# Top-k attention with an MLP behind it: tails of two batches taken together, an even flow of MLP chunks, and two short lists merged by one scan

## The chip, the cores and the metric

The kernel runs on one core of one Trainium2 chip. The metric is the device time of one execution in microseconds (us). TensorE (PE) multiplies, VectorE (DVE), ScalarE (ACT) and GpSimd (POOL) work on vectors, SyncE (SP) issues the transfers.

## What is computed

The reference is sparse attention whose output is fed to an MLP. All arrays are float32.

```python
q, k, v: (8, 8, 576, 64)                       # batch, heads, sequence, head size
scores = matmul(q, k^T) / 8
kth    = 32nd largest score of each row
scores = where(scores >= kth, scores, -1e9)
attn   = softmax(scores)
x      = matmul(attn, v) -> (4608, 512)        # the heads side by side
h      = x @ w_in                              # 512 -> 2048
g      = 0 if h <= -1, h if h >= 1, else (h + 1)^2 / 4
out    = g @ w_out                             # 2048 -> 512
```

## The kernel before

**Steps.** The rows of a batch are cut into four blocks of 128 and a tail of 64. A step takes one block of queries for two heads, so that its score tile is 128 x 2 x 576; for a tail, a step takes two pairs of heads, since 64 rows of two heads fill the 128 partitions. A block has four steps, a tail two, which makes 18 per batch and 144 in all. The list `rounds` (L462-L470) gives the order of blocks: of each two batches the four blocks of the first, its tail, the four blocks of the second, its tail; only for the last two batches do both tails come together.

**What a step does.** TensorE computes the scores (`scores`, L257-L271), ScalarE copies them to SBUF as `s`. VectorE finds the 32nd largest value of each row (`first_top`, L282-L294, and `weights`, L297-L347). It halves the work with pairs: `more` is the larger of columns c and c + 288 (L279); the 32 largest of `more` come by four rounds of MAX8 with MATCH_REPLACE8 between them (L290, L306, L315), in `tops`, falling. Then `more` is overwritten with the smaller of each pair (L317) and its eight largest are `seconds` (L320). The two lists have to be merged: L321 takes the elementwise smaller of `seconds` and the eight values of `tops` just ahead of the last, in reverse order, and L324 takes the largest of these and the 32nd of `tops`, once for each of the two lists. That is the threshold `kth`. L330 keeps the exponentials at or above it and sums them; L335 and L336 give the reciprocal of the sum. ScalarE makes the exponentials ahead of that (L291, L293), GpSimd scales them (L343) and notes by how much the eighth of `seconds` exceeds the threshold (L345); if that ever happened, a second, plain version of the whole computation would run behind the first.

**From weights to the MLP.** The scaled weights are transposed by a transfer (`move_w`, L368-L375) or, in the first and the last steps, by TensorE (`transpose_w`, L351-L364). `values` (L381-L404) multiplies them with v into `xT`, the MLP's input. When the steps of all tiles of a chunk are through, the chunk's MLP is pending (L606-L608): 16 slices of the hidden layer, each with L419 on TensorE, L423 and L431 on ScalarE, L436 to L438 on GpSimd, and L444 on TensorE four slices behind. A chunk is one tile of 128 rows or a pair of tiles; two tails of 64 rows make one tile. Pairs use products with 256 columns at L419, single tiles 128. In the last chunk, VectorE takes over GpSimd's part (L426-L430).

**Who orders the work.** Everything on the four compute engines runs in the order in which the program is written, and a planner in the kernel writes it. For each step it goes through seven slots (L629-L669). In each it emits a part of the top-k work, perhaps scores, values or transposes of neighbouring steps, and then calls `advance` (L516-L532) with an allowance of products. An allowance is counted in units of a 128 x 128 x 128 product; a tile has 128 units, and `pending` pieces are emitted while the amount due covers their cost. The allowance per step, `share`, is all the products not yet emitted, of ready and of future chunks, over the steps that are left (L619). `K_TIME` (L513) is the planner's idea of the length of a step on VectorE. During the first 14 steps or so the weights w_in and w_out are also converted piece by piece.

```python
            share = (total - spent) / (n + 2 - m)
...
                advance((EARLY_SHARE if early else share) / SLOTS if m < n else 32.0, now)
```

Of the kernel before, what the change touches and what calls it, by code (L numbers as in the profile page):

```python
# [10 lines left out]
F32 = mybir.dt.float32  # L11
# [13 lines left out]
def kernel(  # L25
# [10 lines left out]
    nc = tc.nc  # L36
    B, H, S, D = q.shape
    NTOK, DM = out.shape
    DFF = moe_w_in.shape[1]
    P = 128  # L40
# [4 lines left out]
    NT = S // P  # L45
# [6 lines left out]
    NK = DM // P  # L52
    NF = DFF // P
# [5 lines left out]
    const = ctx.enter_context(tc.tile_pool(name="const", bufs=1))  # L59
# [18 lines left out]
    for i in range(2):  # L78
        v_tails.append([const.tile([P, H, D], F32, name=f"v_tail{i}{x}") for x in range(2)])
        for x in v_tails[i]:  # L80
            nc.gpsimd.memset(x, 0.0)

# [5 lines left out]
    excess = const.tile([P, 2 * n_steps + n_pieces], F32, name="excess")  # L88
# [68 lines left out]
    def run(ctx, paired):  # L157
        xtp = ctx.enter_context(tc.tile_pool(name="xtp", bufs=3))
        stage = ctx.enter_context(tc.tile_pool(name="stage", bufs=2))
        att = ctx.enter_context(tc.tile_pool(name="att", bufs=2))  # L160
# [96 lines left out]
        def scores(st):  # L257
            t, hp, kT, qT = st["t"], st["hp"], st["keys"]["kT"], st["qT"]
            st["s"] = s = att.tile([P, 2, S], F32, name="s", bufs=3)
            for hf in range(2):  # L260
# [9 lines left out]
                                             start=True, stop=True)  # L270
                nc.scalar.activation(s[:, :, c0:c1], sp[:, :, 0:SH], AF.Copy, scale=SCALE)  # L271

        def pairs(st):
            s = st["s"]
            st["more"] = more = att.tile([P, 2, SH], F32, name="more")
            nc.vector.tensor_tensor(out=more, in0=s[:, :, 0:SH], in1=s[:, :, SH:S], op=ALU.max)  # L279


        def first_top(st):  # L282
            s = st["s"]
            if paired:
                pairs(st)
            st["tops"] = tops = att.tile([P, 2, TOP_K + 8], F32, name="tops", bufs=3)
            st["e"] = e = att.tile([P, 2, S], F32, name="e", bufs=3)
            nmax = att.tile([P, 2], F32, name="nmax")
            for i in range(2):
                nc.vector.max(out=tops[:, i, 0:8], in_=(st["more"] if paired else s)[:, i, :])  # L290
            nc.scalar.activation(nmax, tops[:, :, 0], AF.Copy, scale=-1.0)  # L291
            for i in range(2):
                nc.scalar.activation(e[:, i, :], s[:, i, :], AF.Exp, bias=nmax[:, i:i + 1])  # L293
                yield  # L294


        def weights(st, after):  # L297
            s, m, tops, e = st["s"], st["m"], st["tops"], st["e"]
            kth = att.tile([P, 2, 8], F32, name="kth", bufs=3)
            if paired:  # L300
                src = rest = less = st["more"]
            else:
                src, rest = s, att.tile([P, 2, S], F32, name="rest", bufs=1)
            for r in range(8, TOP_K, 8):
                for i in range(2):
                    nc.vector.match_replace(out=rest[:, i, :], in_to_replace=tops[:, i, r - 8:r],  # L306
                                            in_values=src[:, i, :], imm_value=LOWEST)
                src = rest
                if r == 8:
                    yield  # L310
                if r + 8 == TOP_K:
                    yield
                    yield from first_top(after) if after is not None else (None, None)
                for i in range(2):
                    nc.vector.max(out=tops[:, i, r:r + 8], in_=src[:, i, :])  # L315
            if paired:
                nc.vector.tensor_tensor(out=less, in0=s[:, :, 0:SH], in1=s[:, :, SH:S], op=ALU.min)  # L317
                seconds = att.tile([P, 2, 8], F32, name="seconds")
                for i in range(2):
                    nc.vector.max(out=seconds[:, i, :], in_=less[:, i, :])  # L320
                nc.vector.tensor_tensor(out=tops[:, :, TOP_K:TOP_K + 8], in0=tops[:, :, TOP_K - 2:TOP_K - 10:-1],  # L321
                                        in1=seconds, op=ALU.min)
                for i in range(2):
                    nc.vector.max(out=kth[:, i, :], in_=tops[:, i, TOP_K - 1:TOP_K + 8])  # L324
                last = kth[:, :, 0]
            else:
                last = tops[:, :, TOP_K - 1]
            z = att.tile([P, 2], F32, name="z")
            for i in range(2):
                nc.vector.scalar_tensor_tensor(out=e[:, i, :], in0=s[:, i, :], scalar=last[:, i:i + 1],  # L330
                                               in1=e[:, i, :], op0=ALU.is_ge, op1=ALU.mult,
                                               accum_out=z[:, i:i + 1])
            yield
            rz = att.tile([P, 2], F32, name="rz")
            nc.vector.tensor_scalar(z, z, 1e-9, None, ALU.add)  # L335
            nc.vector.reciprocal(rz, z)  # L336
            if st["by_tensor"]:
                st["rz"] = diag = (late or words).tile([P, 2, P], F32, name="diag", bufs=1)
                for i in range(2):
                    nc.scalar.activation(diag[:, i, :], ident, AF.Copy, scale=rz[:, i:i + 1])  # L340
            else:
                for i in range(2):
                    nc.gpsimd.tensor_scalar(e[:, i, :], e[:, i, :], rz[:, i:i + 1], 1.0, ALU.mult, ALU.mult)  # L343
            if paired:
                nc.gpsimd.tensor_tensor(out=excess[:, 2 * m:2 * m + 2], in0=seconds[:, :, 7], in1=kth[:, :, 0],  # L345
                                        op=ALU.subtract)
            yield  # L347

# [113 lines left out]
        rounds, chunks = [], []  # L462
        for b in range(0, B, 2):
            a, c, tl = [(b, t) for t in range(NT)], [(b + 1, t) for t in range(NT)], (b, NT)
            if b + 2 < B:
                rounds += a + [tl] + c + [(b + 1, NT)]
                chunks += [a[0:2], a[2:4], c[0:2], c[2:4], [tl]] if b else [[x] for x in a + c + [tl]]
            else:
                rounds += a + [tl, (b + 1, NT)] + c
                chunks += [a[0:2], a[2:4], [tl]] + [[x] for x in c]  # L470
        steps = []
        for b, t in rounds:
            tile_of = (b, t) if t < NT else (b - b % 2, t)
# [4 lines left out]
        n = len(steps)  # L478

        ready = {max(m for m in range(n) if steps[m][3] == ch): ch for ch in range(len(chunks))}  # L480
# [4 lines left out]
        pending = deque()  # L485
        total, spent = sum(len(tiles) for tiles in chunks) * (NK * NF + NF * DM // P), 0
# [23 lines left out]
                inspected += 1  # L510


        K_TIME, PIECE_TIME, UNIT_TIME, SLOTS, EARLY_STEPS, EARLY_SHARE = 10.2, 0.55, 0.218, 7, 4, 32  # L513
        pe_time, dve_time, done, scored, ready_at, usable = 9.0, 12.0, {}, {}, {}, {0: 0.0}

        def advance(amount, until):  # L516
# [95 lines left out]
        for m in range(n + 2):  # L612
# [3 lines left out]
            elif not early and late is None:  # L616
                conversion.close()
                late = ctx.enter_context(tc.tile_pool(name="late", bufs=1))
            share = (total - spent) / (n + 2 - m)  # L619
            top_k, parts = None, [0] * SLOTS  # L620
            if m < n:
                top_k = weights(state[m], state[m + 1] if m + 1 < n else None)
                parts = [1] * SLOTS if early else [1, 1, 0, 1, 1, 1, 1]
                start = max(dve_time, scored[m])
                now_converting = range(SLOTS) if m < EARLY_STEPS else range(0, SLOTS, 2)
                dve_time = start + K_TIME + PIECE_TIME * min(len(now_converting), n_pieces - converted)
                done[m] = dve_time
                state[m]["by_tensor"] = early or m >= n - 2
# [93 lines left out]
```

## Time and profile before

The median of three runs is 1683.67 us (1682.41 to 1685.46). The profiled execution has a span of 1683.5 us.

| engine | busy us | share of the span |
|---|---|---|
| VectorE | 1550.5 | 92% |
| TensorE, products | 1549.2 | 92% |
| ScalarE | 1188.2 | 71% |
| TensorE, weight loads | 1050.8 | 62% |
| GpSimd | 974.8 | 58% |

The costliest groups of VectorE are L306 with 375.6 us, L315 with 348.9 and L330 with 242.0; L321 has 32.6 us in 144 instructions and L324 34.6 us in 288. Of TensorE, L419 has 594.1 us and L444 564.3. In the page, matmuls are pipelined and their ends are modelled, so that a record's duration is no price; the distance from the start of one record to the start of the next is. A product in float32 leaves two records. A group line has the line number, engine, operation, what is written and read with shapes, the count, then busy time and mean duration. A line of the timeline begins with the start and the duration in us; "x8" are eight records merged. A line of waits names who waited for whom, then us in total, times, and the longest.

### The profile page before, as it was taken

Reading aid. Unit: us, or ns where it says so; the run is one execution under the profiler, and the core shown is the slowest. Engines: PE = TensorE matmul, PEld = TensorE weight load, DVE = VectorE, ACT = ScalarE, POOL = GpSimd, SP = SyncE. Lnnn points to the kernel's source line nnn. Section 1 sums busy time; section 2 is a strip of 40 time slices with the busy share of each in tenths; the row PEclk is TensorE's granted clock in tenths of the full one; section 3 lists DMA queues with packets and bytes.
Section 4 is the critical chain, followed back from the end, with each engine's and each line's share of the span. In section 5 each row is a group of like instructions: output and inputs, shape, how many; then the busy total and the mean of one; then the engine's idle time right before and its main releaser. Section 6 shows DMA issues by size and latency. Waiting matters only on the chain.

```text
span 1683.5 us, 30910 instructions
## 1 busy us (share of the span) xinstructions
PE 1549.2 (92%) x9645; PEld 1050.8 (62%) x9645; DVE 1550.5 (92%) x4875; ACT 1188.2 (71%) x2552; POOL 974.8 (58%) x1720
## 2 busy tenths in 40 slices
PE   5586999999998899979999999979999999999998
PEld 4464666666665666646566766646566666666675
DVE  6999999999999999999999999999999999999922
ACT  5677677777777767777677877767667877767743
POOL 4675677666665554536465755526465765657750
PEclk6698999999998999979999999979999999999999
DMA  9333345455555546554555555554555544544400
GB/s 246 114 98 91 86 132 160 129 151 141 140 154 156 144 135 174 142 157 135 146 159 143 150 142 151 158 158 124 155 150 151 143 131 130 132 133 117 114 27 16
DMA packets 439055, 227.83 MB, mean 135 GB/s; under 512 B 393056, under 2 KB 401248, under 8 KB 438880
## 3 DMA queue, kind: packets, MB, share of 16 engines
q1 hardware_dynamic: 438880, 225.75, 49.4%
q8 instruction: 78, 1.28, 0.3%
q14 instruction: 97, 0.79, 0.2%
HBM read 62.91 MB, written 86.11 MB: 89 GB/s over the span
## 4 chain that ended last, share of the span: by engine, by line
DVE 51%; PE 33%; ACT 7%; issue 3%; POOL 3%; DMA 2%; SPq 1%; DVEq 0%; POOLq 0%; ACTq 0%
PE ph L419 13%; DVE more L306 12%; PE py L444 12%; DVE tops L315 10%; DVE e L330 8%; DVE more L317 4%; DVE seconds L320 4%; DVE tops L290 4%; DVE more L279 4%; PE po L389 3%; PE sp L269 3%; ACT halves L372 2%; ACT e L293 1%; DVE z L335 1%; DVE kth L324 1%
## 5 line engine op out<-in xcount | busy, mean ns | idle before, releaser
L419 PEld LDWEIGHTS ph<-xT,w_in 128*128 128x128 f32 x3328 | 505.1, 195 | 199.0 <-issue 88.5
L419 PE MATMUL ph<-xT,w_in 128*128 128x128 f32 (+1 forms) x3328 | 594.1, 326 | 32.8 <-ACT g L431 18.6
L444 PE MATMUL py<-w_out,g 128*128 128x512 f32 x1152 | 564.3, 605 | 2.0 <-POOL w_out L136 1.8
L423 ACT ACTIVATE r<-ph,half 128x128 f32<-128x128 f32 (+1 forms) x416 | 169.7, 408 | 292.9 <-PE ph L419 237.6
L306 DVE MATCH_REPLACE8 more<-tops,more 128x288 f32<-128x288 f32 x864 | 375.6, 442 | 0.0
L436 POOL TENSOR_SCALAR r<-r 128x128 f32<-128x128 f32 (+1 forms) x392 | 164.9, 421 | 343.4 <-ACT r L423 342.1
L315 DVE MAX8 tops<-more 128x8 f32<-128x288 f32 x864 | 348.9, 445 | 0.0
L343 POOL TENSOR_SCALAR e<-e,rz 128x576 f32<-128x576 f32 x260 | 211.9, 825 | 205.2 <-DVE rz L336 205.2
L372 ACT COPY halves<-e 128x1152 uint16<-128x1152 uint16 x260 | 286.9, 1156 | 14.7 <-POOL e L343 14.0
L444 PEld LDWEIGHTS py<-w_out,g 128*128 128x128 f32 x1152 | 197.4, 191 | 145.9 <-issue 117.8
L438 POOL TENSOR_TENSOR g<-r,g 128x128 f32<-128x128 f32 (+1 forms) x400 | 261.6, 654 | 31.4
L330 DVE SCALAR_TENSOR_TENSOR e<-s,kth,e 128x576 f32<-128x576 f32 x288 | 242.0, 877 | 0.5
L437 POOL TENSOR_TENSOR r<-r 128x128 f32<-128x128 f32 (+1 forms) x392 | 219.0, 559 | 32.7
L293 ACT ACTIVATE e<-s,nmax 128x576 f32<-128x576 f32 x288 | 218.4, 771 | 4.8
L269 PE MATMUL sp<-kT,qT 64*128 64x288 f32 x1024 | 169.0, 447 | 9.9 <-ACT kT L229 9.1
L271 ACT ACTIVATE s<-sp 128x576 f32<-128x576 f32 x288 | 170.0, 642 | 6.6 <-PE sp L269 6.4
L389 PE MATMUL po<-wT,v_in 128*64 128x128 f32 x2048 | 148.5, 287 | 22.1 <-DMA wT<-rows 13.9
L389 PEld LDWEIGHTS po<-wT,v_in 128*64 128x64 f32 x2048 | 115.5, 141 | 80.7 <-issue 18.3
L431 ACT ACTIVATE g<-ph,minus 128x128 f32<-128x128 f32 (+1 forms) x400 | 162.4, 406 | 0.0
L269 PEld LDWEIGHTS sp<-kT,qT 64*128 64x128 f32 x1024 | 91.8, 193 | 84.6 <-issue 40.6
L320 DVE MAX8 seconds<-more 128x8 f32<-128x288 f32 x288 | 118.3, 452 | 13.9
L317 DVE TENSOR_TENSOR more<-s 128x576 f32<-128x576 f32 x144 | 122.4, 850 | 4.9
(88 smaller groups left out, 1349.6 us busy)
## 6 DMA issues: line engine op xcount, KB each, us to landing
rows<-halves SPq DMA_DIRECT2D x130, 576.0 KB, 2.8
raw<-in_moe_w_out_dram SPq DMA_DIRECT2D x52, 256.0 KB, 3.0
raw<-in_moe_w_in_dram SPq DMA_DIRECT2D x48, 256.0 KB, 3.1
k_in<-in_k_dram SPq DMA_DIRECT2D x64, 128.0 KB, 2.9
q_in<-in_q_dram SPq DMA_DIRECT2D x32, 256.0 KB, 3.1
v_in<-in_v_dram SPq DMA_DIRECT2D x8, 1024.0 KB, 6.0
out_dram<-y SPq DMA_DIRECT2D x32, 256.0 KB, 2.6
kT<-in_moe_w_in_dram SPq DMA_DIRECT2D x16, 256.0 KB, 4.5
```

Of the source, the lines that this page charges most:

```text
L269: nc.tensor.matmul(o[:, a0 - c0:a1 - c0], qT[d, g, :], kT[d, g, k0:k0 + a1 - a0], start=True, stop=True)
L293: nc.scalar.activation(e[:, i, :], s[:, i, :], AF.Exp, bias=nmax[:, i:i + 1])
L306: nc.vector.match_replace(out=rest[:, i, :], in_to_replace=tops[:, i, r - 8:r], in_values=src[:, i, :], imm_value=LOWEST)
L315: nc.vector.max(out=tops[:, i, r:r + 8], in_=src[:, i, :])
L330: nc.vector.scalar_tensor_tensor(out=e[:, i, :], in0=s[:, i, :], scalar=last[:, i:i + 1], in1=e[:, i, :], op0=ALU.is_ge, op1=ALU.mult, acc ...
L343: nc.gpsimd.tensor_scalar(e[:, i, :], e[:, i, :], rz[:, i:i + 1], 1.0, ALU.mult, ALU.mult)
L372: nc.scalar.copy(halves[:, :, i * S:(i + 1) * S], st["e"][:, i, :].bitcast(U16).rearrange("p (k t) -> p t k", t=2))
L389: nc.tensor.matmul(po[j * D:(j + 1) * D], v_in[:, h, c, :] if c < NT else v_tl[0][:, h, :], wT[:, block(j, c)], start=(c == 0), stop=(c == ...
L419: nc.tensor.matmul(ph, w_in[:, kk, f * P:(f + 1) * P], xT[:, kk, c0:c1], start=(kk == 0), stop=(kk == NK - 1))
L437: nc.gpsimd.tensor_tensor(out=r, in0=r, in1=r, op=ALU.mult)
L438: nc.gpsimd.tensor_tensor(out=g, in0=r, in1=g, op=ALU.add)
L444: nc.tensor.matmul(pys[i], gs[f][:, i * P:(i + 1) * P], w_out[:, f, :], start=(f == 0), stop=(f == NF - 1))
```

## The change

Four things. The tails of two batches are now taken one behind the other everywhere, after the four blocks of the first, so that the tile they share is ready in the middle of the two batches rather than at their end. The chunks are cut anew: of the four pairs of batches, the first and the last have single tiles throughout, the second has pairs, the third has pairs in its first batch and single tiles in its second. The allowance `share` gets an upper limit, so that what is ready lasts until the next chunk is ready, and the same for every later chunk. And the two lists are merged by one scan: `tops` of the two rows of a step are laid out so that the end of the first list and the second half of the second lie side by side, `seconds` gets a large value in front of each list and is read backwards, and a scan with max and then min runs over 25 elements; its elements 8 and 24 are the two thresholds.

```diff
+    SPLIT = TOP_K // 2
+    LAST = SPLIT + 8
+    second_lists = [const.tile([P, LAST + 1], F32, name=f"seconds{i}") for i in range(2)]
+    for x in second_lists:
+        nc.gpsimd.memset(x, LOWEST)
+        for i in range(2):
+            nc.gpsimd.memset(x[:, i * SPLIT:i * SPLIT + 1], LARGEST)
...
+        def eight(tops, i, r):
+            c = (r // SPLIT * 2 + i) * SPLIT + r % SPLIT
+            return tops[:, c:c + 8]
...
-            nc.scalar.activation(nmax, tops[:, :, 0], AF.Copy, scale=-1.0)
+            nc.scalar.activation(nmax, tops[:, 0:2 * SPLIT:SPLIT], AF.Copy, scale=-1.0)
...
                 for i in range(2):
-                    nc.vector.max(out=seconds[:, i, :], in_=less[:, i, :])
-                nc.vector.tensor_tensor(out=tops[:, :, TOP_K:TOP_K + 8], in0=tops[:, :, TOP_K - 2:TOP_K - 10:-1],
-                                        in1=seconds, op=ALU.min)
-                for i in range(2):
-                    nc.vector.max(out=kth[:, i, :], in_=tops[:, i, TOP_K - 1:TOP_K + 8])
-                last = kth[:, :, 0]
+                    nc.vector.max(out=seconds[:, (1 - i) * SPLIT + 1:(1 - i) * SPLIT + 9], in_=less[:, i, :])
+
+                nc.vector.tensor_tensor_scan(out=kth, data0=tops[:, 2 * TOP_K - 1 - LAST:2 * TOP_K], data1=seconds[:, LAST::-1],
+                                             initial=LOWEST, op0=ALU.max, op1=ALU.min)
+                last = [kth[:, 8:9], kth[:, LAST:LAST + 1]]
...
-            if b + 2 < B:
-                rounds += a + [tl] + c + [(b + 1, NT)]
-                chunks += [a[0:2], a[2:4], c[0:2], c[2:4], [tl]] if b else [[x] for x in a + c + [tl]]
+            rounds += a + [tl, (b + 1, NT)] + c
+            if 0 < b and b + 2 < B:
+                chunks += [a[0:2], a[2:4], [tl]] + ([c[0:2], c[2:4]] if b + 4 < B else [[x] for x in c])
             else:
-                rounds += a + [tl, (b + 1, NT)] + c
-                chunks += [a[0:2], a[2:4], [tl]] + [[x] for x in c]
+                chunks += [[x] for x in a + [tl] + c]
...
-        K_TIME, PIECE_TIME, UNIT_TIME, SLOTS, EARLY_STEPS, EARLY_SHARE = 10.2, 0.55, 0.218, 7, 4, 32
+        K_TIME, PIECE_TIME, UNIT_TIME, SLOTS, EARLY_STEPS, EARLY_SHARE = 10.4, 0.55, 0.218, 7, 4, 32
...
-            share = (total - spent) / (n + 2 - m)
+            share, left = (total - spent) / (n + 2 - m), sum(x[0] for x in pending)
+            for r in sorted(ready):
+                if r + 3 > m and r >= valued:
+                    share = min(share, left / (r + 3 - m))
+                    left += len(chunks[ready[r]]) * (NK * NF + NF * DM // P)
```

More of the change, by code (lines that the diff above doesn't have):

```diff
@@ L285, in first_top @@
                 pairs(st)
-            st["tops"] = tops = att.tile([P, 2, TOP_K + 8], F32, name="tops", bufs=3)
+            st["tops"] = tops = att.tile([P, 2 * TOP_K], F32, name="tops", bufs=3)
             st["e"] = e = att.tile([P, 2, S], F32, name="e", bufs=3)
@@ L289, in first_top @@
             for i in range(2):
-                nc.vector.max(out=tops[:, i, 0:8], in_=(st["more"] if paired else s)[:, i, :])
-            nc.scalar.activation(nmax, tops[:, :, 0], AF.Copy, scale=-1.0)
+                nc.vector.max(out=eight(tops, i, 0), in_=(st["more"] if paired else s)[:, i, :])
+            nc.scalar.activation(nmax, tops[:, 0:2 * SPLIT:SPLIT], AF.Copy, scale=-1.0)
             for i in range(2):
@@ L298, in weights @@
             s, m, tops, e = st["s"], st["m"], st["tops"], st["e"]
-            kth = att.tile([P, 2, 8], F32, name="kth", bufs=3)
+            kth = att.tile([P, LAST + 1], F32, name="kth", bufs=3)
             if paired:
@@ L305, in weights @@
                 for i in range(2):
-                    nc.vector.match_replace(out=rest[:, i, :], in_to_replace=tops[:, i, r - 8:r],
+                    nc.vector.match_replace(out=rest[:, i, :], in_to_replace=eight(tops, i, r - 8),
                                             in_values=src[:, i, :], imm_value=LOWEST)
@@ L314, in weights @@
                 for i in range(2):
-                    nc.vector.max(out=tops[:, i, r:r + 8], in_=src[:, i, :])
+                    nc.vector.max(out=eight(tops, i, r), in_=src[:, i, :])
             if paired:
                 nc.vector.tensor_tensor(out=less, in0=s[:, :, 0:SH], in1=s[:, :, SH:S], op=ALU.min)
-                seconds = att.tile([P, 2, 8], F32, name="seconds")
+                seconds = second_lists[m % 2]
                 for i in range(2):
-                    nc.vector.max(out=seconds[:, i, :], in_=less[:, i, :])
-                nc.vector.tensor_tensor(out=tops[:, :, TOP_K:TOP_K + 8], in0=tops[:, :, TOP_K - 2:TOP_K - 10:-1],
-                                        in1=seconds, op=ALU.min)
-                for i in range(2):
-                    nc.vector.max(out=kth[:, i, :], in_=tops[:, i, TOP_K - 1:TOP_K + 8])
-                last = kth[:, :, 0]
+                    nc.vector.max(out=seconds[:, (1 - i) * SPLIT + 1:(1 - i) * SPLIT + 9], in_=less[:, i, :])
+                nc.vector.tensor_tensor_scan(out=kth, data0=tops[:, 2 * TOP_K - 1 - LAST:2 * TOP_K], data1=seconds[:, LAST::-1],
+                                             initial=LOWEST, op0=ALU.max, op1=ALU.min)
+                last = [kth[:, 8:9], kth[:, LAST:LAST + 1]]
             else:
-                last = tops[:, :, TOP_K - 1]
+                last = [eight(tops, i, TOP_K - 8)[:, 7:8] for i in range(2)]
             z = att.tile([P, 2], F32, name="z")
             for i in range(2):
-                nc.vector.scalar_tensor_tensor(out=e[:, i, :], in0=s[:, i, :], scalar=last[:, i:i + 1],
+                nc.vector.scalar_tensor_tensor(out=e[:, i, :], in0=s[:, i, :], scalar=last[i],
                                                in1=e[:, i, :], op0=ALU.is_ge, op1=ALU.mult,
@@ L344, in weights @@
             if paired:
-                nc.gpsimd.tensor_tensor(out=excess[:, 2 * m:2 * m + 2], in0=seconds[:, :, 7], in1=kth[:, :, 0],
+                nc.gpsimd.tensor_tensor(out=excess[:, 2 * m:2 * m + 2], in0=seconds[:, 8:9 + SPLIT:SPLIT], in1=kth[:, LAST:7:-SPLIT],
                                         op=ALU.subtract)
```

## The prediction, made before the changed kernel ran

> **What bounds the kernel now.** I read the page's busy row and slices first, then the chain of waits, then a table of stretches, then the timeline of single steps. A step is one pass of VectorE over one score tile; there are 144. I cut the span where the timeline shows the thresholding instruction L330 of steps 14, 45 and 100, and where VectorE ends.
>
> ```profile
> PE 1549.2 (92%) x9645; PEld 1050.8 (62%) x9645; DVE 1550.5 (92%) x4875; ACT 1188.2 (71%) x2552; POOL 974.8 (58%) x1720
> DVE  6999999999999999999999999999999999999922
> PEclk6698999999998999979999999979999999999999
> DVE 51%; PE 33%; ACT 7%; issue 3%; POOL 3%; DMA 2%; SPq 1%; DVEq 0%; POOLq 0%; ACTq 0%
> ```
>
> VectorE is busy in every slice but the last two, where TensorE works alone. The chain agrees: half of it is VectorE, a third TensorE. The PEclk dips are the places where TensorE had run out of products. The table of stretches (busy us per engine, then clock, DMA share, GB/s):
>
> ```profile
> 0.00:211.00 211.00, 150.12 (x960) 112.14 (x961) 193.02 (x576) 142.99 (x351) 128.51 (x210) 0.82 0.45 127
> 211.00:554.00 343.00, 320.22 (x2264) 220.71 (x2263) 325.35 (x1028) 258.83 (x584) 228.50 (x450) 0.97 0.55 147
> 554.00:1141.00 587.00, 554.40 (x3185) 362.96 (x3185) 569.70 (x1812) 422.58 (x837) 313.10 (x509) 0.95 0.55 148
> 1141.00:1606.00 465.00, 454.31 (x2814) 304.54 (x2812) 450.47 (x1422) 336.05 (x702) 284.18 (x498) 0.99 0.50 135
> 1606.00:1684.00 78.00, 70.16 (x433) 50.45 (x431) 11.99 (x42) 27.70 (x82) 20.55 (x55) 0.97 0.04 13
> ```
>
> VectorE is busy 95 to 97% of the three middle rows, which is as dense as its steps get. Call the rows A (steps 0-13), B (14-44, 31 steps), C (45-99, 55 steps), D (100-142, 43 steps) and tail. From L330 of one step to the next the timeline gives 342.3/31 = 11.04 us in B, 587.9/55 = 10.69 in C and 463.8/43 = 10.78 in D. The shortest step, seen many times where no products ran, is 10.36. So 0.33 to 0.68 us a step is stretch, and the question is what stretches it.
>
> ```profile
> DVE more L279 <- ACT s L271: 8.0, 9, 2.1
> 331.37 1.96 POOL L343 TENSOR_SCALAR e<-e,rz 128x576 f32<-128x576 f32 x2
> 331.44 1.27 DVE L317 TENSOR_TENSOR more<-s 128x576 f32<-128x576 f32 x1
> ```
>
> The first line, from the waits of stretch B, says VectorE waited 8.0 us for scores there, 0.26 a step (1.6 us after 550 in all). The other two show the larger part: L317, 0.76 us at its median, lasts 1.27 while GpSimd works on e. Such collisions are hidden inside busy time.
>
> [...] py records average 605 ns, but a pair of them, one product, advances the timeline by 0.86 us. So I price TensorE by starts.
>
> **The merge by scan.** Once a step VectorE runs L321 and two L324 between the last L320 and the first L330:
>
> ```profile
> 905.78 0.17 DVE L321 TENSOR_TENSOR tops<-tops,seconds 128x16 f32<-128x16 f32 x1
> 905.99 0.24 DVE L324 MAX8 kth<-tops 128x8 f32<-128x9 f32 x2
> 906.19 0.82 DVE L330 SCALAR_TENSOR_TENSOR e<-s,kth,e 128x576 f32<-128x576 f32 x1
> ```
>
> That is 0.41 us from start to start. In its place comes one scan over 25 elements. [...] the 0.04 us gap to the instruction that reads its result (905.95 to 905.99) stays: 0.25. Saving 0.16 a step. Bounds: 0.20 if it cost what L321 costs, zero if it had another 0.16 of fixed cost. I take 0.16[...]. It adds no wait: the first L330 now waits for both lists' seconds, but these already stood before it on the same engine. The reads of strided columns (nmax, excess) keep their 2 elements, and the added memsets lie on GpSimd before its first work: nothing. The K_TIME change is in the planner only and costs no instruction.
>
> **The tails together and the sharing out.** No product is added. What moves is when TensorE is given them; I read it from the order of instructions on TensorE in both builds, which is fixed. Prices, from starts in the timeline: a product of L419 with 128 columns 0.224 us (1549.05 to 1549.94 for four), with 256 columns 0.432 (1048.85 to 1050.58 for four), of L444 0.86. A tile alone is 64 x 0.224 + 16 x 0.86 = 28.1; two together 64 x 0.432 + 32 x 0.86 = 55.2. The change has six pairs instead of ten: 4 x 1.0 = 4 us more for TensorE, which has room. Everything else on TensorE is some 2.7 us a step (scores 1.17, values 1.24, transposes). Products in us per step, before and after: A 1.9 and 1.9; B 7.2 and 6.7; C 6.5 and 7.0; D 7.3 and 7.5. Behind the last scores, L269 of step 143: before 164 of L419 and 46 of L444, 76.3 us; after 132 and 37, 61.4. Once products have begun, six steps before have none at all, for lack of a ready chunk (45, 46, 63, 64, 99, 100); after, every step has some.
>
> Tail. Before, the last L269 starts at 1586.67 and TensorE ends at 1676.96, 90.3 later; the prices give 76.3 + 1.2 scores + 6.2 values + 4.5 transposes of the last weights + 2.1 left for gaps, 90.3. It is dense, so the tail is TensorE's own: 14.9 us of products fewer bring the end 14.9 us closer to the last L269, if VectorE's last weights arrive in time. After, they are wanted about 24 us behind that L269, and before they were ready about 22 behind it: in time, barely. The copy, store and finish behind (6.5 us) stay.
>
> Stages, as shifts of that last L269. A: 14 x 0.16 = -2.2. B: fewer products per step, so part of the wait for scores goes (0.26 to about 0.1) and collisions shrink with GpSimd's share, 0.42 x 6.7/7.2 = 0.39; step 10.20 + 0.49 = 10.69 against 11.04, 31 x -0.35 = -10.9. C: 7% more products, stretch 0.33 to 0.35, step 10.55: 55 x -0.14 = -7.7. D is where I chose. Before, D is mostly pairs; after, all 43 steps have single tiles, whose GpSimd work per tile is, by the mean durations of L436 to L438, 16 x (0.38 + 0.46 + 0.54) = 22 us against 8 x (0.48 + 0.71 + 0.82) = 16 for a tile of a pair, and whose L423/L431 chain has half the time per product. Single tiles ran before in B at 0.68 us of stretch and in steps 134-142 at about 0.48 (10.84 a step, at 7.7 us of products). I take the middle, 0.58: step 10.78, shift zero. TensorE's load there is 7.5 + 2.7 = 10.2, just below. Sum -20.8; with the tail -14.9: 1683.7 - 35.7 = 1648.
>
> **The rivals.** First, D stays as light as C (10.6 a step, -7.7) and B loses all its waits (10.59, a further -3): 1637. For it: an even flow hits fewer full queues, and the DVE waits of late D are nearly nil. Against: GpSimd is busier with single tiles. Second, the scan saves nothing, 143 x 0.16 = +23: 1671; the sharing and the tail remain. For it: no scan is in the trace, and small VectorE instructions have cost floors (165 ns for the two elements of L336). Third, on the other side: the single tiles of D fill ScalarE, GpSimd and TensorE so that scores come late, as at 284.56 in B, and steps go to 11.4 (+0.62 x 43 = +27), and the scan also brings nothing (another +16 outside D, where it no longer counts): 1648 + 43 = 1691, slower. Against it: even B, with these waits, averaged 11.04, and the worst single steps of 12 to 13 us stood alone.
>
> **How the numbers follow.** The forecast 0.55, the first rival 0.25, the second 0.15, the third 0.05. Predicted time 1648. The range reaches down past the first rival (scan at its cheapest end, 143 x 0.04 = 6 us less) to 1632 and up to the second, 1671; some of the forecast's neighbours and the third rival are left out. Slower is the third rival, 0.05. Within 0.2% (3.4 us) is the upper edge of the second, 0.02, which leaves 0.93 for faster.
>
> **What would show it.** The scan as one group of 144 with a mean near 0.22 to 0.26 us, and 0.25 us from its start to L330's. Shortest step 10.20. B at 10.7, C at 10.55, D between 10.6 and 11.0 a step. No PEclk dip in the middle. Last L269 to the end 82 us instead of 97, with TensorE dense. The prediction is wrong if the scan takes over 0.4 us, if D's waits of VectorE for scores exceed 10 us, or if TensorE idles in the tail for the last diag.

## The result, and the profile after

The changed kernel took 1665.63 us (median of 4 runs, 1665.23 to 1668.41) against 1683.04 us for the kernel before on the same chip: a ratio of 0.9898, 95% interval 0.9881 to 0.9915, some 17 us. Forecast were 36: the direction was right, and less than half of the gain came.

The page of the changed kernel, first its busy row, then VectorE and clock by slices, then the chain of waits by engine:

```profile
PE 1540.7 (92%) x10157; PEld 1057.8 (63%) x10157; DVE 1532.8 (92%) x4587; ACT 1208.2 (72%) x2680; POOL 1041.8 (63%) x1918
...
DVE  6999999999999999999999999999989998999942
...
PEclk6798999999999999999999999999999999999999
...
PE 38%; DVE 37%; ACT 14%; POOL 5%; issue 4%; DMA 1%; SPq 0%; POOLq 0%; DVEq 0%; ACTq 0%
```

Three things are new. The granted clock no longer dips in the middle: its means in B, C and D are 0.99, 0.99 and 1.00, where before they were 0.97, 0.95 and 0.99. TensorE has products throughout; before, from 720 to 735 us, it was busy 7.66 of the 15 us, at a mean clock of 0.63. Last, VectorE's row has an eight in slices 30 and 34, which it had nowhere before. In the chain VectorE fell from 51% to 37%, while ScalarE went from 7% to 14%, GpSimd from 3% to 5% and TensorE from 33% to 38%. Where this happened shows when the chain is cut by stretch: in D it was 74% VectorE and 21% TensorE before; after, it is 62% TensorE, 25% ScalarE and 9% GpSimd, and VectorE is not in it at all.

With the span cut where the prediction cut it (L330 is now L344), the stages come out like this; a shift is against the kernel before, for the tail from the last score products (L269, now L279) to the end:

| stage | us a step before | after | shift forecast | shift measured |
|---|---|---|---|---|
| A, steps 0-13 | 12.94 | 12.78 | -2.2 | -2.3 |
| B, 14-44 | 11.04 | 10.70 | -10.9 | -10.6 |
| C, 45-99 | 10.69 | 10.51 | -7.7 | -9.6 |
| D, 100-142 | 10.79 | 11.21 | 0 | +18.4 |
| tail | 96.8 in all | 84.1 in all | -14.9 | -12.7 |

Four of the five terms are within 2.2 us. The whole miss is stretch D. Here is that stretch in the table of stretches (the row of before, 465 us long with VectorE busy 450.5 of them, is in the prediction), and in it VectorE's waits and TensorE's for ScalarE (before, then after):

```profile
1119.00:1602.00 483.00, 459.91 (x3233) 318.52 (x3232) 448.59 (x1332) 356.75 (x824) 341.75 (x682) 1.00 0.48 130
```

```profile
DVE more L279 <- ACT s L271: 1.2, 1, 1.2
PE ph L419 <- ACT g L431: 4.3, 6, 1.5
PE po L389 <- ACT g L431: 2.1, 1, 2.1
...
DVE more L294 <- ACT s L281: 20.6, 16, 3.9
PE ph L433 <- ACT g L445: 16.9, 23, 1.8
PE po L403 <- ACT g L445: 5.2, 5, 2.2
```

VectorE is busy for as long as before (448.6 us against 450.5) in a stretch 18 us longer. What grew is its idle time: it waited 20.6 us for scores that ScalarE had not yet copied, where before it was 1.2 us. TensorE's load did not change: at the prediction's prices, the products that start in D come to 7.42 us a step before and 7.45 after. But TensorE now waits 22.1 us for ScalarE instead of 6.4. ScalarE is busy 74% of the stretch instead of 72, GpSimd 71% instead of 61. The largest of these waits, in the timeline (start, duration, engine, line; what ended the idle time in brackets):

```profile
1218.23 0.85 POOL L452 TENSOR_TENSOR g<-r,g 128x128 f32<-128x128 f32 x1
1218.70 0.99 DVE L344 SCALAR_TENSOR_TENSOR e<-s,kth,e 128x576 f32<-128x576 f32 x1
1219.06 0.79 POOL L450 TENSOR_SCALAR r<-r 128x128 f32<-128x128 f32 x1
1219.12 0.37 ACT L437 ACTIVATE r<-ph,half 128x128 f32<-128x128 f32 x1 [3.16 <-POOL g L452]
...
1219.79 1.16 PE L433 MATMUL ph<-xT,w_in 128*128 128x128 f32 x8 [1.76 <-ACT g L445]
...
1220.88 1.24 PE L279 MATMUL sp<-kT,qT 64*128 64x288 f32 x8
...
1221.42 2.20 ACT L386 COPY halves<-e 128x1152 uint16<-128x1152 uint16 x2
...
1224.44 0.51 ACT L163 ACTIVATE sign<-raw,tiny 128x256 f32<-128x256 f32 x1
...
1226.09 0.77 ACT L308 ACTIVATE e<-s,nmax 128x576 f32<-128x576 f32 x1
...
1226.76 1.18 ACT L281 ACTIVATE s<-sp 128x576 f32<-128x576 f32 x2
...
1227.97 0.76 DVE L294 TENSOR_TENSOR more<-s 128x576 f32<-128x576 f32 x1 [3.87 <-ACT s L281]
```

The reader sees a chain through four engines. GpSimd's L452 and L450 last 0.85 and 0.79 us, where their medians are 0.46 and 0.29, while VectorE's L344 runs (0.93 and 0.99 us, where its median is 0.82). ScalarE's L437 needs the scratch tile r back from GpSimd and stands still for 3.16 us. TensorE's next slice waits for ScalarE (1.76 us). The score products end at 1222.1, but ScalarE is behind by then: it works without a pause through the copies for the transpose, two exponentials, the inspection of a piece of the weights (L163) and a slice of the MLP, and copies the scores only at 1226.76. VectorE had been idle for 3.87 us.

A word on that inspection. The weights reach the kernel as 64-bit numbers, not as float32 as the section on what is computed has it: a transfer of 256 KB brings 128 x 256 of them. They are converted during the first steps; later, in every second step, they are loaded once more and ScalarE checks their size.

The scan itself, by group (count, busy us and mean ns), and by its minimum, median and maximum:

```profile
L337 DVE TENSOR_TENSOR_SCAN kth<-tops,seconds 128x25 f32<-128x25 f32 x144 | 40.5, 281 | 4.9
```

```profile
L337 DVE TENSOR_TENSOR_SCAN kth<-tops,seconds x144: 210/212/657, 30.0 to 1601.0; 128x25 f32<-128x25 f32 x144
```

The prediction's 0.25 us is a gap of 0.04 and 0.21 for the scan itself. The gap is in the trace of before; the 0.21 was not shown there, since no scan runs in it, and was the author's assumption (L321, with 16 elements, has a median of 0.175 us). The trace after agrees with it: the scan's median is 212 ns. From its start to that of L344 it is 0.25 us at the median, as forecast, against 0.42 for the merge of before. The shortest step fell from 10.36 to 10.20 us, as forecast. The mean, 281 ns, is above the median because the scan, too, gets longer beside GpSimd: in the 61 cases in which no GpSimd instruction overlaps it, it takes 215 ns at most, in the other 83 it has a mean of 332.

### The profile page after: what moved, and what is told of

It is laid out like the page before. It is cut to its first block, busy times and chain, and to the rows that moved or that the text cites. A ratio compares the mean times of both kernels' runs of the same rounds, so it can differ in the third digit from the quotient of the medians.

```text
span 1666.6 us, 32108 instructions
## 1 busy us (share of the span) xinstructions
PE 1540.7 (92%) x10157; PEld 1057.8 (63%) x10157; DVE 1532.8 (92%) x4587; ACT 1208.2 (72%) x2680; POOL 1041.8 (63%) x1918
## 4 chain that ended last, share of the span: by engine, by line
PE 38%; DVE 37%; ACT 14%; POOL 5%; issue 4%; DMA 1%; SPq 0%; POOLq 0%; DVEq 0%; ACTq 0%
PE ph L433 15%; PE py L458 14%; DVE more L321 9%; DVE tops L330 8%; DVE e L344 6%; ACT halves L386 4%; PE sp L279 4%; PE po L403 4%; DVE seconds L335 3%; DVE more L332 3%; DVE tops L305 3%; ACT e L308 3%; DVE more L294 3%; POOL e L357 2%; ACT s L281 2%
## 5 line engine op out<-in xcount | busy, mean ns | idle before, releaser
L433 PEld LDWEIGHTS ph<-xT,w_in 128*128 128x128 f32 x3840 | 531.0, 193 | 222.7 <-issue 99.6
L433 PE MATMUL ph<-xT,w_in 128*128 128x128 f32 (+1 forms) x3840 | 604.6, 304 | 47.2 <-ACT g L445 43.4
L458 PE MATMUL py<-w_out,g 128*128 128x512 f32 x1152 | 573.4, 604 | 1.7 <-POOL w_out L146 0.9
L450 POOL TENSOR_SCALAR r<-r 128x128 f32<-128x128 f32 (+1 forms) x456 | 187.0, 410 | 408.7 <-ACT r L437 407.6
L437 ACT ACTIVATE r<-ph,half 128x128 f32<-128x128 f32 (+1 forms) x480 | 186.9, 389 | 273.9 <-PE ph L433 228.0
L321 DVE MATCH_REPLACE8 more<-tops,more 128x288 f32<-128x288 f32 x864 | 375.7, 442 | 0.0
L330 DVE MAX8 tops<-more 128x8 f32<-128x288 f32 x864 | 349.1, 445 | 0.0
L452 POOL TENSOR_TENSOR g<-r,g 128x128 f32<-128x128 f32 (+1 forms) x464 | 277.6, 598 | 36.4
L458 PEld LDWEIGHTS py<-w_out,g 128*128 128x128 f32 x1152 | 192.4, 191 | 117.6 <-issue 87.9
L451 POOL TENSOR_TENSOR r<-r 128x128 f32<-128x128 f32 (+1 forms) x456 | 239.2, 525 | 38.0
L344 DVE SCALAR_TENSOR_TENSOR e<-s,kth,e 128x576 f32<-128x576 f32 x288 | 249.9, 904 | 6.0
L445 ACT ACTIVATE g<-ph,minus 128x128 f32<-128x128 f32 (+1 forms) x464 | 179.6, 387 | 0.0
L279 PE MATMUL sp<-kT,qT 64*128 64x288 f32 x1024 | 163.1, 436 | 9.4 <-ACT kT L239 8.5
L403 PE MATMUL po<-wT,v_in 128*64 128x128 f32 x2048 | 143.9, 280 | 16.5 <-ACT g L445 11.3
L279 PEld LDWEIGHTS sp<-kT,qT 64*128 64x128 f32 x1024 | 90.2, 189 | 84.3 <-issue 52.3
L294 DVE TENSOR_TENSOR more<-s 128x576 f32<-128x576 f32 x144 | 112.4, 780 | 23.9 <-ACT s L281 23.5
```

What stands on the lines that cost most here:

```text
L279: nc.tensor.matmul(o[:, a0 - c0:a1 - c0], qT[d, g, :], kT[d, g, k0:k0 + a1 - a0], start=True, stop=True)
L321: nc.vector.match_replace(out=rest[:, i, :], in_to_replace=eight(tops, i, r - 8), in_values=src[:, i, :], imm_value=LOWEST)
L330: nc.vector.max(out=eight(tops, i, r), in_=src[:, i, :])
L403: nc.tensor.matmul(po[j * D:(j + 1) * D], v_in[:, h, c, :] if c < NT else v_tl[0][:, h, :], wT[:, block(j, c)], start=(c == 0), stop=(c == ...
L433: nc.tensor.matmul(ph, w_in[:, kk, f * P:(f + 1) * P], xT[:, kk, c0:c1], start=(kk == 0), stop=(kk == NK - 1))
L451: nc.gpsimd.tensor_tensor(out=r, in0=r, in1=r, op=ALU.mult)
```

## The experiments

My theory after the result: the single tiles of D are what makes it slow, since each costs ScalarE and GpSimd more for the same products, and the scores stand in ScalarE's queue. Rivals: TensorE's load of 10.2 us a step; the faster VectorE itself, which collides more; the even flow, which leaves no pause to catch up. Each run is compared with the kernel before on the same chip; the kernels of one group ran together.

### The scan alone, and the flow alone

The first kernel has only the scan; TensorE's order is that of before. The second has the rounds, chunks, limit and K_TIME of after with the merge of before. In brief, as steps back from the changed kernel:

```text
 scan alone                                      flow alone
-  rounds, chunks, limit, K_TIME of after        -  tensor_tensor_scan(out=kth, ...)
+  rounds, chunks, share, K_TIME of before       +  tensor_tensor(min); max for each list
```

> The kernel before with the merge by scan only; rounds, chunks, allowance and K_TIME as before, so TensorE's order of instructions is that of before. Scan costs as priced (0.25 us in place of 0.41 from start to start): VectorE, which bounds A to D, gains 0.16 a step and the end follows the last scores, about -20 us (1663). If stretch D is held by something other than VectorE, as it seems to be after the change, D gains nothing: about -14 us (1669). If a shorter step on VectorE only makes the others collide more: within 5 us of before.

> The change without the scan: rounds, chunks, allowance and K_TIME of after, merge as before. Theory (stretch D is held by the chain of single tiles, not by VectorE): D takes 11.2 us a step as after the whole change, B, C and A lose the 0.16 a step that the scan gave, about 15 us together, so 1680. Rival (D is slow because the faster VectorE collides with the others): D near 10.8, so the whole is 1680 + 15 - 17 = 1678 but with D under 10.9. If the flow alone brings all and the scan nothing: 1666.

Measured: the scan alone 1673.65 us, ratio 0.9943 (0.9921 to 0.9964); the flow alone 1681.93, ratio 0.9990 (0.9983 to 0.9997). Per stage, against before:

| | A | B | C | D | tail |
|---|---|---|---|---|---|
| scan alone | -1.9 | -2.4 | -5.0 | -3.0 | -0.3 |
| flow alone | -0.8 | -8.6 | -0.3 | +18.9 | -12.5 |
| both | -2.3 | -10.6 | -9.6 | +18.4 | -12.7 |

D is slow without the scan as well: the rival of the faster VectorE falls. The flow gains 21 us in B and the tail and loses 19 of them in D, so that alone it is worth two. The scan, priced at 23 us, gives about 10 alone and about 15 on top of the flow. Its 0.16 us shows in full in the shortest step (10.20) but not in the mean, and the groups of VectorE in the run of the scan alone say where some of the rest went:

```profile
L344 DVE SCALAR_TENSOR_TENSOR e<-s,kth,e 128x576 f32<-128x576 f32 x288 | 247.0, 894 | 6.0
L332 DVE TENSOR_TENSOR more<-s 128x576 f32<-128x576 f32 x144 | 124.5, 864 | 4.9
...
L294 DVE TENSOR_TENSOR more<-s 128x576 f32<-128x576 f32 x144 | 115.4, 802 | 12.1 <-ACT s L281 11.6
L337 DVE TENSOR_TENSOR_SCAN kth<-tops,seconds 128x25 f32<-128x25 f32 x144 | 39.0, 271 | 4.9
```

Before, the first three had means of 877, 850 and 792 ns. L344 runs twice a step, so these are 2 x 17 + 14 + 10 = 58 ns a step, 8 us in the run, longer. Their shapes, and so their work, are the same. The trace shows where they got longer: the half of the L344 that overlaps no GpSimd instruction has a mean of 816 ns in both runs and never exceeds 821, the other half went from 937 to 970. So about a third of the saving, 58 of 160 ns a step, came back as longer instructions; for L344 the trace shows that it was beside GpSimd.

### Pairs of tiles in D

```diff
-            if 0 < b and b + 2 < B:
-                chunks += [a[0:2], a[2:4], [tl]] + ([c[0:2], c[2:4]] if b + 4 < B else [[x] for x in c])
-            else:
-                chunks += [[x] for x in a + [tl] + c]
+            if b == 0:
+                chunks += [[x] for x in a + [tl] + c]
+            else:
+                chunks += [a[0:2], a[2:4], [tl]] + ([c[0:2], c[2:4]] if b + 2 < B else [[x] for x in c])
```

> The change, with the third pair of batches in pairs of tiles throughout and the last in pairs in its first batch, so ten pairs as before the change; products in D 7.3 us a step instead of 7.5, behind the last scores 70 us instead of 61. Theory (the width of single tiles makes D slow): D at 10.6 a step, 26 us less, tail 9 us longer: about 1650. Rival (TensorE's load makes D slow): D gets only the 8 us of products less, the tail takes them back: about 1666. Rival (the even flow itself, no pause in which GpSimd and ScalarE catch up): D stays at 11.2, with the tail 1675.

1644.42 us, ratio 0.9765 (0.9744 to 0.9787): 22 us faster than the changed kernel. Stretch D in this run, and VectorE's waits for scores in it:

```profile
1115.00:1569.00 454.00, 442.57 (x2665) 294.62 (x2662) 440.14 (x1331) 328.79 (x682) 274.64 (x475) 0.99 0.51 136
```

```profile
DVE more L294 <- ACT s L281: 0.5, 1, 0.5
```

D takes 10.55 us a step and is 28.3 us shorter than after the change; the waits are gone (20.6 to 0.5 us), VectorE is busy 97% of it. ScalarE has 28 us less to do in D, GpSimd 67 us less. The products in D differ by some 8 us between the two kernels, so TensorE's load can't be more than a third of the gain. The run of the scan alone says the same: its D, mostly pairs, has the load of after (7.42 us of products a step) and is 21 us shorter. The rule by which products are shared out is the same with late pairs as after: grouping the tiles in pairs is what cures most of D. In the chain of this stretch VectorE is back with 40%. A pair differs from two single tiles in two ways, fewer and wider instructions on ScalarE and GpSimd, and an arrival half as often; this run does not separate them, the next three bear on the first. The tail gives 7 us back, since 70 us of products instead of 61 are left behind the last scores.

### Which of the engines holds the single tiles

Three runs loosen one link each: a third buffer for r, less ScalarE, less GpSimd. The second leaves out the two sums that judge the weights; the third leaves out the square for single tiles after the conversion, and so computes something else.

```diff
-                r = pool.tile([P, CW], F32, name="r", bufs=2)[:, 0:c1 - c0]
+                r = pool.tile([P, CW], F32, name="r", bufs=3)[:, 0:c1 - c0]
```

> The change, with three buffers instead of two for r, the scratch tile that ScalarE writes and GpSimd reads. Theory in its narrow form (single tiles: ScalarE stands still behind GpSimd because r has only two buffers, and the score copies stand behind it): D's waits of ScalarE for GpSimd (14 us) go, VectorE's waits for scores fall from 20.6 to under 10, D gains 8 to 12 us: about 1656. Rival (ScalarE itself or TensorE is full there): no change, 1666 within 2 us.

```diff
+    nc.gpsimd.memset(signs, 0.0)
...
-        for x in range(2):
-            sign = pool.tile([P, WC], F32, name="sign", bufs=1)
-            nc.scalar.activation(sign, hi.bitcast(F32), AF.Sign, bias=tiny[:, x:x + 1],
-                                 accum_out=signs[:, x, i:i + 1])
+        sign = pool.tile([P, WC], F32, name="sign", bufs=1)
+        nc.scalar.activation(sign[:, 0:1], hi[:, 0:1].bitcast(F32), AF.Sign)
```

> The change, with ScalarE's inspection of the raw weights cut to one element per partition (the two sums that judge the weights are left out, the loads stay): 1.2 us less of ScalarE every second step, 0.6 a step, nothing less for the other engines. If ScalarE's own load makes scores late in D, D falls by about its 0.4 a step (17 us) and B a little: about 1648. If the wait is GpSimd's, through r, ScalarE only waits longer: under 5 us gained, 1662 or more. If TensorE is full: no change.

```diff
                     nc.gpsimd.tensor_scalar(r, r, 1.0, 0.0, ALU.min, ALU.max)
-                    nc.gpsimd.tensor_tensor(out=r, in0=r, in1=r, op=ALU.mult)
+                    if converted < n_pieces or len(tiles) > 1:
+                        nc.gpsimd.tensor_tensor(out=r, in0=r, in1=r, op=ALU.mult)
```

> The change, with the square on GpSimd (one of its three instructions per slice) left out for single tiles once the weights are converted; the output differs there. GpSimd has 4.2 x 0.5 = 2 us less a step in D. If GpSimd's chain behind single tiles is what holds D, D falls to the pairs' 10.55 (28 us) and B by 5 to 8: about 1632. If ScalarE or TensorE holds D: collisions on VectorE fall (0.1 to 0.2 a step in B and D), so about 1655 at best.

| run | us, ratio (interval) | D, us a step | shift of D against after | VectorE's waits for scores, whole run |
|---|---|---|---|---|
| after | 1665.63, 0.9898 (0.9881 to 0.9915) | 11.21 | | 23.5 |
| three r | 1655.90, 0.9835 (0.9815 to 0.9855) | 11.06 | -6.5 | 14.6 |
| less ScalarE | 1649.25, 0.9798 (0.9782 to 0.9814) | 10.90 | -13.6 | 6.9 |
| less GpSimd | 1652.03, 0.9822 (0.9800 to 0.9844) | 11.03 | -7.8 | 18.2 |
| pairs | 1644.42, 0.9765 (0.9744 to 0.9787) | 10.55 | -28.3 | 3.1 |

No single link holds D. All three help, none restores the 10.55 of the pairs. ScalarE's time weighs most: 0.50 us less a step in D (0.6 were expected) brings 0.31, while 2.06 us less of GpSimd bring 0.18. Of the expectations, the one that GpSimd's chain alone holds D (1632) was wrong, and so was "under 5 us gained" for the short inspection; that ScalarE's own load makes the scores late (1648) came nearly true, with 13.6 us in D instead of 17. That TensorE is full, so that nothing would change, fell. The third buffer brought the total that was expected (1656), but for other reasons in part: D gave 6.5 us instead of 8 to 12, and VectorE's waits there fell to 13.5 us, not under 10; the rest came mostly from B and C. Its waits, by line, show that it shortened ScalarE's stops behind GpSimd rather than removed them (the longest 2.2 us instead of 3.2):

```profile
ACT r L437 <- POOL g L452: 30.0, 25, 2.2
```

What is not settled: the last nine steps of D (134-142), single tiles as well, took 10.70 us after the change, and only the 34 ahead of them took 11.35. ScalarE has 0.4 us a step less to do in the nine (8.0 against 8.4): no keys of a further batch are copied, and fewer pieces of the weights inspected. Cutting the inspection brought the 34 to 10.99. But TensorE has fewer products in the nine as well (7.3 us a step against 7.5), and no run separates the two.

### The limit, the place of the tails, the planner's step

```diff
-            share, left = (total - spent) / (n + 2 - m), sum(x[0] for x in pending)
-            for r in sorted(ready):
-                ...
+            share = (total - spent) / (n + 2 - m)
```

> The change without the upper limit of the allowance: new rounds and chunks, the scan, K_TIME of after, and share as before the change. Products per step then are B 7.2 as before (6.7 with the limit), C 6.8, D 7.5; behind the last scores 56 us instead of 61. If the limit is what made B faster (8.6 us in the run of the flow alone), B goes back to 10.95 a step (+8) and C and D stay; the tail is 5 us shorter: about 1669. If the tails' place and not the limit did it, B stays: about 1661.

1703.41 us, ratio 1.0116 (1.0096 to 1.0135): without the limit the change would have made the kernel slower, by 20 us. The expected 1669 was far off. Not only B is slow (11.35 a step), C and D are too (10.76 and 11.40). The products that start in each stretch are nearly the same as with the limit, in B as well: 6.71, 7.03 and 7.48 us a step in B, C and D against 6.61, 6.98 and 7.45. The waits of this run:

```profile
DVE more L294 <- ACT s L281: 54.1, 40, 4.0
ACT r L437 <- POOL g L452: 50.8, 43, 3.6
...
PE ph L433 <- ACT g L445: 30.7, 43, 2.0
```

VectorE waits for scores 40 times instead of 20, ScalarE for GpSimd 50.8 us instead of 27.1. The mean load of a stretch doesn't say this; it is how the products lie within it. Without the limit a fresh chunk is emitted faster than the next one comes, and then there is too little. The trace shows the bunching: the products that start in one step vary with a standard deviation of 2.3, 1.4 and 1.8 us in B, C and D, against 0.8, 0.9 and 0.9 with the limit, and in B three steps have less than 2 us of them. That the bunches are what makes the queues overflow remains argued.

```text
 scan, limit and K_TIME of after;
-  rounds, chunks of after
+  rounds, chunks of before (tails apart except in the last pair, ten pairs of tiles)
```

> The scan, the limit of the allowance and K_TIME of after, but rounds and chunks of before: the tails of two batches apart except in the last pair, ten pairs. Against the scan alone (1673.7) it adds the limit; against the run with late pairs (1644.4) it takes back the tails together. Products per step B 6.6, C 6.7, D 7.6, 72 us behind the last scores. If the limit does the work and the place of the tails little: 1648. If the tails together are what makes the arrival even enough: D is overloaded at 7.6 + 2.7 = 10.3 us of TensorE a step, 11.0, and the whole about 1660.

1662.05 us, ratio 0.9874 (0.9857 to 0.9890). Against the scan alone the limit, with K_TIME of after, brings 12 us with the old rounds. Against the run with late pairs, which has the same ten pairs, the tails apart cost 18 us, 16 of them in D (10.92 a step with 7.6 us of products). The place of the tails does count, as the second half of the expectation said: pairs alone don't make D light. How much of the 16 us is the larger load (7.3 us of products with late pairs) and how much the place of the tails, is not separated.

```diff
-        K_TIME, ... = 10.4, ...
+        K_TIME, ... = 10.2, ...
```

> The change with the planner's K_TIME left at 10.2. It moves some products by a place in TensorE's order and adds none: 1666 within 3 us. If the planner's idea of the step matters to where products meet the scores in D: more than 5 us either way.

1669.18 us, ratio 0.9917 (0.9901 to 0.9934). The interval overlaps that of the changed kernel; the medians are 3.5 us apart, which is not told apart from none.

### The merge of before with pairs, and the fastest version

```text
 pairs in D as above;
-  tensor_tensor_scan(out=kth, ...)
+  tensor_tensor(min); max for each list
```

> The flow with pairs in the third pair of batches and the last, as in the run with late pairs, but with the merge of before (no scan). Theory (the scan's 0.16 us a step counts where VectorE bounds the step and is lost where scores come late): with pairs C and D are VectorE's, so the merge of before costs 9 us in C, 7 in D, 2 each in A and B, 20 together: 1644 + 20 = 1664. Rival [...]: 12 us, 1656.

1660.91 us, ratio 0.9867 (0.9850 to 0.9883). With pairs the scan is worth 16.5 us by the medians, 17 by the ratios: between the two expectations (in the second, half of what VectorE saves is lost again beside GpSimd), so this doesn't decide between them. By stage, from the two profiled executions, it is 12.2 in C, 4.9 in D, 2.1 in A, 0.5 in B. The 12.2 are more than the 55 x 0.16 = 8.8 that the shorter merge can give there by itself and B kept almost nothing: a shorter merge also shifts what meets on the engines, so the stages don't say how much of the 0.16 us a stretch keeps.

The last run has more pairs, in the second batch of the first two as well, and the third buffer. Against the run with late pairs:

```diff
-            if b == 0:
-                chunks += [[x] for x in a + [tl] + c]
-            else:
-                chunks += [a[0:2], a[2:4], [tl]] + ([c[0:2], c[2:4]] if b + 2 < B else [[x] for x in c])
+            a = [a[0:2], a[2:4]] if b else [[x] for x in a]
+            chunks += a + [[tl]] + ([c[0:2], c[2:4]] if b + 2 < B else [[x] for x in c])
...
-                r = pool.tile([P, CW], F32, name="r", bufs=2)[:, 0:c1 - c0]
+                r = pool.tile([P, CW], F32, name="r", bufs=3)[:, 0:c1 - c0]
```

> The change with pairs wherever the weights are there in time (second batch of the first two, all of the third pair of batches, first batch of the last) and three buffers for r; products in B 6.6 a step, C 6.9, D 7.3, behind the last scores 69 us. Theory (width of the tiles and r are the cause, partly the same one): B at 10.5 instead of 10.7 (6 us less than with pairs in D only), D at 10.5 as there, the rest equal: about 1636. If r's third buffer adds its full 10 us on top: 1630. If pairs in B do nothing: 1643.

1641.04 us, ratio 0.9750 (0.9734 to 0.9766), the fastest of all and ahead of both kernels; the run with late pairs alone can't be told from it, since the intervals overlap. B falls to 10.49 a step, as expected, 7 us less, but C gives 4 us back (10.52 against 10.44). In D the third buffer adds nothing to the pairs (10.56 against 10.55): the two largely cure the same thing there.

## Why the prediction was wrong, point by point

**The bound.** That VectorE bounds the middle and TensorE the tail was right for the kernel before, and for A and C after. In D the chain after the change runs through TensorE, ScalarE and GpSimd, with the scores late behind them. The prediction named this, with the right releaser, in its third rival, but at a chance of 0.05. One of its signs of being wrong came true: VectorE's waits for scores in D are 20.6 us, where it had set 10.

**The step that failed** is the stretch of D: "I take the middle, 0.58: step 10.78, shift zero." Measured were 11.21 less 10.20, 1.01 us of stretch, above both of the values between which I chose (0.48 and 0.68). The lower value was a poor witness: steps 134-142 ran at 10.70 after the change too, and it is the 34 steps ahead of them that took 11.35. And B's 0.68 came with fewer products than D was to have: 7.2 us a step by the prediction's count, 6.7 by the trace, against 7.5. A bound from above was needed, and the run of the flow alone shows that the term was flow +19, where the working had flow +7 and scan -7. What it had missed is a wait, not a longer VectorE: 19 us more of waiting for scores, behind a ScalarE that is itself held by GpSimd and by its own queue.

**The scan's price was right, its worth was not.** 0.25 us for 0.41 holds to 10 ns at the median, and the shortest step shows it. What failed is the multiplication by all steps (0.16 x 143 = 23): measured 10 alone, 15 with the flow, 17 with pairs. In D it brought 0.5 us because VectorE was waiting anyway (20.6 us for scores); in the run of the scan alone a third of it, 58 of 160 ns a step, went into longer instructions, and for L344 these lay beside GpSimd.

**B was right in part by luck.** -10.9 forecast, -10.6 measured, but the flow gave 8.6 and the scan 2.0, where the working had 6 and 5. And its reason, fewer products in B (7.2 to 6.7 us a step), did not come about: the trace has 927 records of L419 and 240 of L444 in B before, 927 and 235 of the same two lines (L433, L458) after. The prediction had counted by the scores' place in TensorE's order, and scores run two steps ahead, so that two empty steps which run in B were counted to C. What changed is the spread: before, single steps of B had from nothing to 9.9 us of products, with the flow alone 5.6 to 7.9, and VectorE's 8.0 us of waits for scores in B fell to none. That is nearly the whole 8.6. C: the flow -0.3 and the scan 9.3, as worked out within 2 us.

**The tail** was right in kind and nearly in size: 84.1 us from the last scores against 82. The rest is new gaps of TensorE, 1.8 us behind ScalarE, most of it here at 1593.84, and 0.2 us for the last diag, which the prediction had named as a sign of being wrong but which counts for little:

```profile
1590.37 1.95 PE L433 MATMUL ph<-xT,w_in 128*128 128x128 f32 x16
1593.84 1.16 PE L433 MATMUL ph<-xT,w_in 128*128 128x128 f32 x8 [1.52 <-ACT g L445]
...
1609.60 2.05 PE L371 MATMUL pw<-diag,e 128*128 128x128 f32 x16 [0.20 <-ACT diag L354]
```

**The price of a pair.** TensorE loses only 1 us when a pair becomes two single tiles; this the prediction had, and from it concluded too little. The pair's worth is on ScalarE and GpSimd: 16 slices of L437 and L445 take twice 368 + 365 ns for two tiles, 477 + 472 for a pair, so 8 us more per pair lost, and GpSimd 12 us by the means that the prediction quoted.

**The limit.** It was treated as part of an even flow whose effect is the products per stretch. The run without it shows that the spread within a stretch counts at nearly the same mean: 38 us with the new chunks.

## What to carry to other kernels

When two engines are each over 90% busy, a shortened instruction on one is worth its saving only where that engine is the one that ends last; multiply it by the steps of those stretches, not by all. Here 0.16 us over 143 steps was forecast to bring 23 us and brought 10 alone, 15 on top of the flow, 17 with pairs; on top of the flow D, where VectorE was not in the chain, had 0.5 of them. When work is cut finer to spread it, price the cut on the engines that follow, not only on the one that computes: here ScalarE took 368 and 365 ns for a slice of 128 columns, 477 and 472 for one of 256, so that half the width cost 77% of the time. And where one queue serves both a stream of background work and the copy that the bounding engine needs next, judge the background work by how it bunches, since a mean load below the limit still made it wait 20 to 40 times.

## What the runs showed of the hardware that was not expected

A scan over 25 elements in float32, with both inputs in SBUF and one read backwards, has a median of 212 ns. The same instruction on VectorE (the product with the mask, L330 before and L344 after), with the same shapes, has a mean of 877 ns over the whole run before and 904 after, and of 948 ns in D after the change, with 806 at the least; where no GpSimd instruction overlaps it, it never exceeds 820 ns. And 0.50 us a step less of ScalarE, itself busy 74% of the stretch, shortened the step by 0.31 us, although no engine's busy share there was over 96%.
